# ScalarE takes the exponentials of both halves of query tiles 7 to 17 head by head, with the maximum as its bias

## The chip, the cores and the metric

The kernel runs on one core of a Trainium2 chip. The metric is the device time of one execution in microseconds (us); lower is better. TensorE (PE) multiplies matrices into PSUM, which has eight banks; VectorE (DVE), ScalarE (ACT) and GpSimd (POOL) do the elementwise work, and DMA queues move data.

## The reference

Three stages follow one another on 4 batches of 576 tokens. The first is attention with random features, 8 heads of 64, 128 features; the two others are feed-forward layers, one with a mixing over tokens before it, one with a Fourier transform.

```python
def phi(x):
    proj = np.einsum('bhsd,md->bhsm', x, omega)
    sq = np.sum(x * x, axis=-1, keepdims=True) / 2.0
    h = proj - sq
    h = h - np.max(h, axis=-1, keepdims=True)
    return np.exp(h) / np.sqrt(m)
q_p, k_p = (phi(q_s), phi(k_s))
kv = np.einsum('bhsm,bhsd->bhmd', k_p, v)
z = np.sum(k_p, axis=2)
num = np.einsum('bhsm,bhmd->bhsd', q_p, kv)
den = np.einsum('bhsm,bhm->bhs', q_p, z)[..., None] + 1e-06
attn = num / den
...
h = np.maximum(xt @ w_tok1, 0.0) @ w_tok2        # over tokens, per batch
u = x + h.transpose(0, 2, 1)
x = u + np.maximum(u @ w_ch1, 0.0) @ w_ch2
...
mixed = np.real(np.fft.fft(np.fft.fft(x, axis=1), axis=2))
un = normalised(x + mixed)
out = x + mixed + np.maximum(un @ w2_ch1, 0.0) @ w2_ch2
```

The term `sq` falls out of `phi`, since it is the same for all features of a row and the maximum is taken off.

## The kernel before

The order of all instructions on every engine is written out by hand in the program; each engine works its list in that order and waits on semaphores.

**Attention.** The 2304 tokens are 18 tiles of 128 rows. Keys and queries of a tile are worked in two halves g of four heads. A list `order` sets the sequence of these (kind, tile, half) slots; where both kinds are at hand, key and query slots alternate, and a query tile begins with its half 1. In each slot `project` multiplies the transposed tile with omega (six matmuls, line 506) into one PSUM bank; operands are split into a high and a low part, so that three products make one. `split_in` (493, 494) makes these parts some slots ahead: ScalarE casts, GpSimd subtracts. `feature` (520 to 528) takes the row maxima of the four heads on VectorE, negated, and the exponentials. For one part of the slots VectorE adds the negated maxima over all four heads (`df`, line 527) and ScalarE takes one exponential of 128x512 (528); for the other part ScalarE reads the bank itself, head by head, with the maximum as its bias (524). Three slots later a key half is multiplied with v (540); a query half is turned by TensorE (565), copied by ScalarE (574 or 569), and later multiplied with the sums of the keys (582) and divided on VectorE (595 to 602). ScalarE and GpSimd split the result (608, 609), and TensorE turns it (616).

**Banks.** Two banks have the tag H, four the tag A, two hold numerators (N0, N1). Projections, turned tiles and the products of the token mixing (`tok_mix`, 667 and 680, added to `x2` by VectorE at 683) all take turns on A. The bank of a projection comes free when its last reader is done.

**Between the slots** VectorE widens weights of the next layers from 64-bit words into a high and a low float (`widen`, 341 to 372, with one copy on ScalarE at 348). A budget for each slot sets how many of these steps stand there; they are not tied to a time. When a batch is complete, steps of `tok_mix` are mixed in, one each slot or each second slot.

**After attention** come the channel layer (776, 860, 861, 898), the transform and the second feed-forward layer, which are not touched.

The lines that decide who takes the maximum off:

```python
if kind == "q":
    by_act = g == 0
else:
    by_act = (i + g) % 3 != 0 if i < 5 else i + g > 0
```

Of the kernel before, what the change touches and what calls it, by code (L numbers as in the profile page):

```python
# [302 lines left out]
def mix_kernel(ctx: ExitStack, tc: tile.TileContext, qt, kt, va, om, w1, w2, wch, wff, t1, t2, out):  # L303
# [208 lines left out]
    def feature(kind, i, g):  # L512
        p4 = proj.pop((kind, i, g)).rearrange("p (h m) -> p h m", m=M)

        if kind == "q":
            by_act = g == 0
        else:
            by_act = (i + g) % 3 != 0 if i < 5 else i + g > 0
        mx = e0.tile([128, 4, 1], F32, tag="mx", name="mx")
        dve.tensor_reduce(out=mx, in_=p4, axis=AX.X, op=ALU.max, negate=True)  # L520
        f = e0.tile([128, 4, M], F32, tag="f", name="f", bufs=6)
        if by_act:
            for hh in range(4):
                act.activation(out=f[:, hh], in_=p4[:, hh], func=AF.Exp, bias=mx[:, hh])  # L524
        else:
            df = e0.tile([128, 4, M], F32, tag="df", name="df", bufs=2)
            dve.tensor_tensor(out=df, in0=p4, in1=mx.to_broadcast([128, 4, M]), op=ALU.add)
            act.activation(out=f, in_=df, func=AF.Exp)
        ft[kind, i, g] = f
# [251 lines left out]
    def attention():  # L781
# [35 lines left out]
        for n in range(-1, n_all + LAG_X):  # L817
            while loads and at[loads[0]] <= n + AHEAD_LOAD:
                load(*loads.pop(0))
            if n == n_all:  # L820
                enter_mlp()
            if 0 <= n < n_all:
                project(*order[n])
            sums(n)
            queries(n)
            while splits and at[splits[0]] <= n + AHEAD_SPLIT:
                split_in(*splits.pop(0))
            if 0 <= n < n_all:
                feature(*order[n])
            results(n)  # L830
            if n >= 2:

                side.step(0.0 if n < 6 else SLOT0_US if n < 10 else SLOT1_US if n < 36 else SLOT_US)
            if fill and (len(fill) > 3 or n % 2 == 0):
                fill.pop(0)()
            for fn in early[:3]:
                fn()
            del early[:3]
# [759 lines left out]
```

## Time and profile before

| | before |
|---|---|
| median of 3 runs | 954.01 us (952.9 to 954.3) |
| profiled execution, own time | 953.26 us |
| its span in the trace | 951.2 us |
| TensorE busy | 931.4 us |
| VectorE busy | 644.2 us |
| ScalarE busy | 301.3 us |
| GpSimd busy | 118.8 us |

The span runs from the first to the last instruction of the trace; about 2 us of the execution lie outside it. Busy times count overlapping instructions once. The ends of matmuls are modelled, so a busy TensorE can still stand behind a short wait; VectorE's and ScalarE's rows overlap by about 0.1 us from one to the next, since the end of an instruction covers the landing of its result.

### The profile page before, as it was taken

Reading aid. Unit: us, or ns where it says so; the run is one execution under the profiler, and the core shown is the slowest. Engines: PE = TensorE matmul, PEld = TensorE weight load, DVE = VectorE, ACT = ScalarE, POOL = GpSimd, SP = SyncE. Lnnn points to the kernel's source line nnn. Section 1 sums busy time; section 2 is a strip of 40 time slices with the busy share of each in tenths; the row PEclk is TensorE's granted clock in tenths of the full one; section 3 lists DMA queues with packets and bytes.
Section 4 is the critical chain, followed back from the end, with each engine's and each line's share of the span. In section 5 each row is a group of like instructions: output and inputs, shape, how many; then the busy total and the mean of one; then the engine's idle time right before and its main releaser. Section 6 shows DMA issues by size and latency. Waiting matters only on the chain.

```text
span 951.2 us, 14064 instructions
## 1 busy us (share of the span) xinstructions
PE 931.4 (98%) x5344; PEld 829.7 (87%) x5344; DVE 644.2 (68%) x1270; ACT 301.3 (32%) x676; POOL 118.8 (12%) x110
## 2 busy tenths in 40 slices
PE   7999998989999999999999999999999999999998
PEld 7999898878889988888888888889899998899986
DVE  5987999985776687877864577667565457533342
ACT  5885765742122222212221212212311113311121
POOL 3353343321120122011000000000000000000000
PEclk9999999999999999999999999999999999999999
DMA  8665464388889386584155348739776756687764
GB/s 272 221 211 178 143 231 173 122 318 320 341 352 418 100 341 217 191 292 167 67 177 216 139 147 270 246 126 359 266 244 234 238 183 221 221 263 257 252 205 160
DMA packets 68257, 216.47 MB, mean 228 GB/s; under 512 B 5600, under 2 KB 14432, under 8 KB 54240
## 3 DMA queue, kind: packets, MB, share of 16 engines
q1 hardware_dynamic: 60992, 172.40, 51.9%
q0 software_dynamic: 7056, 43.06, 12.3%
q8 instruction: 42, 0.69, 0.3%
q14 instruction: 23, 0.19, 0.1%
q10 hardware_dynamic: 144, 0.13, 0.1%
HBM read 169.30 MB, written 42.47 MB: 223 GB/s over the span
## 4 chain that ended last, share of the span: by engine, by line
PE 89%; DVE 9%; ACT 1%; issue 0%; DMA 0%; DVEq 0%; ACTq 0%
PE H L776 22%; PE A L898 16%; PE A L1470 14%; PE H L1457 12%; PE A L1264 7%; PE A L506 4%; PE H L540 2%; PE N L582 2%; DVE mx L520 2%; PE A L667 1%; PE S L1077 1%; DVE cvo L364 1%; PE A L565 1%; PE S L1090 1%; DVE x L598 1%; DVE cvo L372 1%
## 5 line engine op out<-in xcount | busy, mean ns | idle before, releaser
L776 PE MATMUL H<-uh,w 128*128 128x512 f32 (+1 forms) x800 | 215.3, 355 | 2.1 <-DVE x L683 2.1
L776 PEld LDWEIGHTS H<-uh,w 128*128 128x128 f32 x800 | 136.5, 189 | 22.2 <-DVE x L683 2.3
L860 ACT ACTIVATE hh<-H 128x512 fp32r<-128x512 f32 (+1 forms) x92 | 49.0, 533 | 270.7 <-PE H L776 270.5
L776 PE MATMUL H<-ul,w 128*128 128x512 f32 (+1 forms) x304 | 113.7, 374 | 0.4 <-DVE ul L763 0.4
L898 PE MATMUL A<-hh,w 128*128 128x512 f32 (+1 forms) x480 | 108.7, 369 | 0.0
L861 DVE SCALAR_TENSOR_TENSOR hl<-H,hh 128x512 fp32r<-128x512 f32 (+1 forms) x92 | 55.8, 606 | 64.5 <-ACT hh L860 64.3
L1470 PE MATMUL A<-w2t,b 128*128 128x512 f32 x384 | 99.3, 394 | 0.0
L898 PEld LDWEIGHTS A<-hh,w 128*128 128x128 f32 x480 | 84.3, 189 | 15.0
L1457 PE MATMUL H<-b,w1t 128*128 128x384 f32 x480 | 91.5, 336 | 0.0
L1457 PEld LDWEIGHTS H<-b,w1t 128*128 128x128 f32 x480 | 85.0, 188 | 4.0 <-DVE tmp L1501 0.3
L1470 PEld LDWEIGHTS A<-w2t,b 128*128 128x128 f32 x384 | 70.6, 188 | 11.7
L524 ACT ACTIVATE f<-A,mx 128x128 f32<-128x128 f32 x204 | 58.9, 395 | 31.1 <-DVE mx L520 23.4
L776 PEld LDWEIGHTS H<-ul,w 128*128 128x128 f32 x304 | 57.4, 189 | 9.9 <-DVE ul L763 0.8
L898 PE MATMUL A<-hl,w 128*128 128x512 f32 (+1 forms) x240 | 59.2, 369 | 0.0
L1264 PE MATMUL A<-w,hh 128*128 128x512 f32 x192 | 50.5, 395 | 0.0
L520 DVE TENSOR_REDUCE mx<-A 128x4 f32<-128x512 f32 x70 | 47.6, 681 | 3.7 <-ACT f L524 2.2
L898 PEld LDWEIGHTS A<-hl,w 128*128 128x128 f32 x240 | 42.7, 189 | 7.6
L540 PE MATMUL H<-v,f 128*128 128x65 f32 x320 | 40.5, 272 | 0.4 <-ACT f L524 0.4
L540 PEld LDWEIGHTS H<-v,f 128*128 128x128 f32 x320 | 39.4, 193 | 0.8 <-ACT f L524 0.6
L1264 PEld LDWEIGHTS A<-w,hh 128*128 128x128 f32 x192 | 34.6, 189 | 6.1
L360 DVE SCALAR_TENSOR_TENSOR cvo<-cvy,cvo 128x1024 int32<-128x1024 int32 (+2 forms) x32 | 39.3, 1228 | 0.5
L1462 ACT ACTIVATE b<-tmp 128x384 fp32r<-128x384 f32 x16 | 8.4, 525 | 98.1 <-DVE tmp L1523 98.1
(261 smaller groups left out, 1703.4 us busy)
## 6 DMA issues: line engine op xcount, KB each, us to landing
w<-kept SPq DMA_DIRECT2D x60, 1024.0 KB, 6.8
w2t<-kept SPq DMA_DIRECT2D x55, 512.0 KB, 4.9
w1t<-kept SPq DMA_DIRECT2D x48, 512.0 KB, 5.0
stg<-in_wff_dram POOLq DMA_DIRECT2D x16, 1024.0 KB, 6.8
kept<-cvo POOLq DMA_DIRECT2D x13, 1024.0 KB, 7.3
stg<-in_wch_dram SPq DMA_DIRECT2D x9, 1024.0 KB, 6.1
kept<-cvo POOLq DMA_DIRECT2D x16, 512.0 KB, 7.7
kept<-so SPq DMA_DIRECT2D x16, 512.0 KB, 7.7
```

The costliest lines, as they stand in the source:

```text
L360: dve.scalar_tensor_tensor(out=st["h"], in0=st["y"].bitcast(I32), scalar=-0x80000000, in1=st["h"], op0=ALU.bitwise_and, op1=ALU.bitwise_or)
L506: pe.matmul(out=pj[:, p_ * 256:p_ * 256 + 256], lhsT=a[:, c, :], rhs=w, start=(n == 0), stop=(n == 2), skip_group_check=True)
L520: dve.tensor_reduce(out=mx, in_=p4, axis=AX.X, op=ALU.max, negate=True)
L524: act.activation(out=f[:, hh], in_=p4[:, hh], func=AF.Exp, bias=mx[:, hh])
L540: pe.matmul(out=kvp[b, g][:, hh * 65:hh * 65 + 65], lhsT=ft["k", i, g][:, hh, :], rhs=src["v", i, int(off > 0)][:, 4 * g + hh, :], start=( ...
L776: pe.matmul(out=hb[:, 0:n], lhsT=w(a, kk), rhs=u[:, kk, 0:n], start=(c == 0), stop=(c == 11))
L860: act.activation(out=hh, in_=hb[:, 0:n], func=AF.Relu)
L861: dve.scalar_tensor_tensor(out=hl, in0=hb[:, 0:n], scalar=0.0, in1=hh, op0=ALU.max, op1=ALU.subtract)
L898: pe.matmul(out=acc[i][:, 0:cols], lhsT=a[:, cs], rhs=v, start=(n == 0 and c_ == 0), stop=(n == NCH - 1 and c_ == 2))
L1264: pe.matmul(out=acc[t], lhsT=a[:, t * 128:t * 128 + 128], rhs=w, start=(n == 0 and c_ == 0), stop=(n == NFF - 1 and c_ == 2))
L1457: pe.matmul(out=to, lhsT=w[:, a, cs], rhs=v[:, q], start=(start and n == 0), stop=(n == 5), skip_group_check=True)
L1470: pe.matmul(out=acc[t], lhsT=h[n // 2][:, t * 128:t * 128 + 128], rhs=w[:, n % 2], start=(begins and n == 0), stop=(ends and n == 2))
```

## The change

For query tiles 7 to 17 the condition is now true for both halves. In those tiles half 1 has no `df` on VectorE any more, and its one exponential of 128x512 on ScalarE becomes four of 128x128 that read the bank. Query tiles 0 to 6 and all key tiles stay as they are.

```diff
         if kind == "q":
-            by_act = g == 0
+            by_act = g == 0 or i > 6
         else:
             by_act = (i + g) % 3 != 0 if i < 5 else i + g > 0
```

On VectorE, at half 1 of query tile 7, in the middle of the token mixing of the first batch (A is a bank, mx the maxima; cvo, cvy and stg are buffers of the widening):

```order
 L683 TENSOR_TENSOR x_655<-A,x_655 128x288
 L520 TENSOR_REDUCE mx<-A 128x4
-L527 TENSOR_TENSOR df<-A,mx 128x512
 L368 TENSOR_SCALAR cvy<-cvo 128x1024
 L341 TENSOR_SCALAR cvy<-stg 128x1024
```

The steps of the widening behind the difference now follow the maximum directly; this is so eleven times, and nothing else moves on VectorE.

On ScalarE, at the same place (xh is the high part of a divided tile, qh of a query tile, qpT a turned one):

```order
 L608 CAST xh<-x 128x512 [waits DVE_49]
 L493 CAST qh<-qs 128x512 [waits DMAHW5_49,PE_49,Pool_49]
-L528 ACTIVATE f<-df 128x512 [waits DVE_49]
+L524 ACTIVATE f<-A,mx 128x128 [waits DVE_49]
+L524 ACTIVATE f<-A,mx 128x128 x3
 L574 COPY qpT<-A 128x512 [waits PE_49]
 L621 COPY x_1192<-N 128x4x128 [waits PE_49]
```

Four instructions stand where one stood; the order around them is the same.

On TensorE, where the bank of that half is used next, by a product of the token mixing:

```order
 L616 MATMUL N<-ident,x 128x128 x3
 L582 MATMUL N<-kvs,qpT 128x65 x4
-L680 MATMUL A<-w2hl,h1h 128x288 [waits DVE_49,PE_49]
+L680 MATMUL A<-w2hl,h1h 128x288 [waits DVE_49,Activation_49]
 L680 MATMUL A<-w2hl,h1h 128x288
 L680 MATMUL A<-w2hl,h1l 128x288
 L680 MATMUL A<-w2hl,h1h 128x288 x2
 L680 MATMUL A<-w2hl,h1l 128x288
-L506 MATMUL A<-om_h,qh 128x256 [waits Activation_49]
+L506 MATMUL A<-om_h,qh 128x256 [waits DVE_49]
```

TensorE's order is the same throughout. The bank is now given back by ScalarE and not by VectorE, and the projection behind it takes a bank that VectorE gives back.

## Rows read from the trace of the kernel before

**Rows 1.** The page, busy time of each engine.

```profile
PE 931.4 (98%) x5344; PEld 829.7 (87%) x5344; DVE 644.2 (68%) x1270; ACT 301.3 (32%) x676; POOL 118.8 (12%) x110
```

**Rows 2.** Windows: length, busy of PE, PEld, DVE, ACT, POOL; clock; DMA.

```profile
87.00:110.50 23.50, 21.87 (x179) 20.86 (x177) 22.98 (x47) 14.34 (x39) 9.20 (x6) 1.00 0.46 158
110.50:136.00 25.50, 25.39 (x190) 23.95 (x191) 23.86 (x44) 17.84 (x44) 9.77 (x6) 1.00 0.62 217
136.00:181.00 45.00, 40.45 (x333) 38.56 (x331) 43.89 (x90) 28.63 (x71) 17.63 (x11) 1.00 0.43 158
215.00:950.00 735.00, 731.81 (x3802) 639.75 (x3800) 455.49 (x881) 158.34 (x312) 38.35 (x47) 1.00 0.66 234
```

**Rows 3.** The chain that ended last: start, length, what; its changes of engine.

```profile
87.11 0.19 DVE rd L596
...
110.46 0.98 PE A L506 x6
...
136.09 0.19 DVE rd L596
...
180.92 0.75 PE A L616 x4
```

**Rows 4.** Line 527 by itself, 80 to 215 us: min/median/max, first to last.

```profile
L527 DVE TENSOR_TENSOR df<-A,mx x9: 691/691/693, 90.6 to 179.6; 128x512 f32<-128x512 f32 x9
L527 DVE TENSOR_TENSOR df<-H,mx x2: 692/692/692, 173.6 to 185.0; 128x512 f32<-128x512 f32 x2
```

**Rows 5.** VectorE in order of time: start, length, instruction, idle before it.

```profile
89.93 0.68 DVE L520 TENSOR_REDUCE mx<-A 128x4 f32<-128x512 f32 x1
90.64 0.69 DVE L527 TENSOR_TENSOR df<-A,mx 128x512 f32<-128x512 f32 x1
91.24 0.68 DVE L368 TENSOR_SCALAR cvy<-cvo 128x1024 int32<-128x1024 int32 x1
91.84 1.78 DVE L341 TENSOR_SCALAR cvy<-stg 128x1024 f32<-128x1024 f32 x1
...
96.95 0.68 DVE L520 TENSOR_REDUCE mx<-A 128x4 f32<-128x512 f32 x1
97.54 0.69 DVE L352 TENSOR_SCALAR cvo<-stg 128x1024 int32<-128x1024 int32 x1
...
109.09 0.69 DVE L341 TENSOR_SCALAR cvy<-stg 128x1024 f32<-128x1024 f32 x1
...
115.35 0.69 DVE L527 TENSOR_TENSOR df<-A,mx 128x512 f32<-128x512 f32 x1
...
140.88 1.79 DVE L341 TENSOR_SCALAR cvy<-stg 128x1024 f32<-128x1024 f32 x1
```

**Rows 6.** ScalarE in order of time.

```profile
90.79 0.62 ACT L493 CAST qh<-qs 128x512 fp32r<-128x512 f32 x1 [2.06 <-POOL xl L609]
91.36 0.63 ACT L528 ACTIVATE f<-df 128x512 f32<-128x512 f32 x1
91.90 0.57 ACT L574 COPY qpT<-A 128x512 f32<-128x512 f32 x1
...
97.67 1.14 ACT L524 ACTIVATE f<-A,mx 128x128 f32<-128x128 f32 x4 [0.89 <-DVE mx L520]
98.68 0.60 ACT L574 COPY qpT<-A 128x512 f32<-128x512 f32 x1
```

**Rows 7.** GpSimd in order of time.

```profile
88.81 1.98 POOL L609 TENSOR_TENSOR xl<-x,xh 128x512 fp32r<-128x512 f32 x1 [0.25 <-ACT xh L608]
91.49 1.58 POOL L494 TENSOR_TENSOR ql<-qs,qh 128x512 fp32r<-128x512 f32 x1 [0.70 <-ACT qh L493]
```

**Rows 8.** TensorE in order of time.

```profile
92.35 0.51 PE L680 MATMUL A<-w2hl,h1h 128*128 128x288 f32 x2
...
110.46 0.39 PE L506 MATMUL A<-om_h,qh 128*128 128x256 f32 x1 [0.56 <-ACT f L524]
...
116.35 0.28 PE L506 MATMUL A<-om_h,qh 128*128 128x256 f32 x1
```

## The prediction

> **What bounds the kernel now.** I read the page first: TensorE is busy for 931 us of 951, VectorE for 644, ScalarE for 301 [rows 1]. That says that the kernel belongs to TensorE, and it is an average over stages, so the windows come next. Behind 215 us TensorE is idle for 3 us in 735 [rows 2]; nothing of the change lies there, and that part can only move as a whole. The eleven differences that go lie between 90.6 and 185.7 us [rows 4]. Three stretches of this time differ. From 87 to 110.5 us VectorE is busy for 22.98 us of 23.50 and TensorE for 21.87; from 136 to 181 us VectorE for 43.89 of 45.00 and TensorE for 40.45; between the two TensorE for 25.39 of 25.50 [rows 2]. The chain of waits says the same by another way: it goes over to VectorE at 87.11 and back to TensorE at 110.46, again to VectorE at 136.09 and back at 180.92 [rows 3]. So in the two outer stretches VectorE's list sets the pace, and TensorE waits for banks that VectorE, or ScalarE right behind a maximum, gives back (as at 110.46 us [rows 8]). TensorE's idle time there, 23.50 - 21.87 = 1.63 and 45.00 - 40.45 = 4.55 us, 6.2 in all, is about what a faster VectorE can give back. The ends of matmuls are modelled, and the first matmul behind a wait is drawn 0.39 us long where the usual one has 0.28 [rows 8]; for some dozen waits that hides another 1.3 us, so the ceiling is 7.5 us.
>
> **What is taken away.** A maximum at 89.93 us is followed by the difference at 90.64 and the next work at 91.24, 1.31 us later; without a difference the next work starts 97.54 - 96.95 = 0.59 us behind the maximum [rows 5]. One difference thus takes 0.72 us of VectorE's list: its 0.60 and 0.12 in which it waits for the maximum to land. Eleven make 7.9 us. Only those in the outer stretches count. Two begin in the first, 1.4 us together. Two, the one at 115.35 us and the next, lie where TensorE has no idle time, and are worth nothing: VectorE will just wait there. Six begin between 136 and 181 us, 4.3 us together; the last, at 185.0 us, lies behind the chain's return to TensorE. (That there are nine on A up to 179.6 and two on H from 173.6 to 185.0 us is in [rows 4]; the places in between follow from the list.)
>
> **What is added.** One exponential of 128x512 keeps ScalarE from 91.36 to 91.90, 0.54 us; four of 128x128 from 97.67 to 98.68, 1.01 us [rows 6]. That is 0.47 us more in each tile, 5.2 in all. ScalarE is busy for 14.34 us of 23.50 and 28.63 of 45.00 in the outer stretches [rows 2]; eight of the eleven longer steps, 3.8 us, stand in these two, which have 25 us free, so by the sum there is room. The result is not later: the old way ended 0.69 + 0.63 us and two hand-overs, together 1.38 us, behind the maximum (90.61 to 91.99), the new one ends 1.18 us behind it (97.63 to 98.81) [rows 5, 6].
>
> The bank is. It was free when the difference ended, 0.72 us behind the maximum (91.33); now it is free with the fourth exponential, 1.18 us behind it, 0.46 us later. At 116.35 us TensorE projects into a bank that a difference freed at 115.35 + 0.69 = 116.04 [rows 5, 8]: 0.31 us of slack, so 0.15 us of new wait. At 92.35 us it takes a bank freed at 91.33, 1.02 us of slack [rows 5, 8]; but ScalarE comes to these exponentials only behind a cast that waits for GpSimd, at 91.36 [rows 6], and they will end at 91.36 + 1.14 = 92.50. That delay of about 0.2 us falls in a stretch where TensorE has idle time ahead, and I count it at nothing; without that cover it would cost the 0.2, here and once more at the like place near 141 us.
>
> For ScalarE's price there is a rule in the Trainium skill, "ScalarE: Activation LUTs", Rules for kernel authors: about 0.3 us for each ACTIVATE and 0.83 ns for each element. As an estimate from that page four of 128 take 1.6 us and one of 512 takes 0.7, a surcharge of 0.9 us where the row has 0.47; the banks would be held 0.5 us longer still, and the sum below would come to about 4.4 us. Successive ACTIVATEs overlap in the rows, which the rule doesn't count.
>
> **The sum.** First stretch: 1.4 - 0.15 = 1.25 us. Second stretch: 4.3 us, of which I take 3.5. The last tiles have no key slots between their own and follow each other closely (three differences from 173.6 to 185.0 us [rows 4]); there ScalarE's 0.47 each falls on a shorter stretch and the banks are wanted sooner; 0.5 for one bank held longer and 0.3 for ScalarE's queue is what I take off, an estimate from the 0.46 and 0.47. Together 4.75 us.
>
> **GpSimd** moves this either way. The widening at 91.84 us takes 1.78 us, and 0.69 us when GpSimd is idle [rows 5]; GpSimd's subtraction begins at 91.49 [rows 7]. It happens once more at 140.88 (1.79 us). The difference and the maximum are not stretched by GpSimd's work up to 90.79 us. Four of the eight differences that count stand ahead of such widening steps, two in each outer stretch, and now the widening runs up against GpSimd at other moments. It can lose the whole 0.72 us, four times, 2.9 us, when it only waits for GpSimd's end instead of for the difference; or it can win 1.1 us twice. At the first place the step at 91.24 would start at about 90.5, wait until 90.79, and the one behind it would begin at about 91.3, 0.2 us ahead of GpSimd's start at 91.49, which is tied to ScalarE's cast and not to VectorE. So I take it to get through, but at a lead of 0.2 us only, and what it wins is capped by TensorE's idle time left (1.63 - 1.25 and 4.55 - 3.5 = 1.4 us). I add 0.6 us, a little under half of that.
>
> The sum is 5.4 us, against the profiled execution 953.26 - 5.4 = 947.9 us; that execution lies 0.75 us under the median of 954.01, so the forecast is 948.6 us. By the bounds of the parts the gain is 4.75 - 2.9 = 1.9 us at least and 7.5 at most.
>
> **Rivals.**
> 1. *Banks come back later.* Every second slot a bank is held 0.46 us longer. Where ScalarE comes late to the exponentials, TensorE waits, and a part of the gain is only moved from VectorE's waits to ScalarE's. For it: the slack of 0.31 at 116.35, and the late start at 91.36. Against it: the other slack of 1.02, and exponentials that now start 0.7 us earlier. If four of the eight tiles of the outer stretches lose 0.5 us, 2 us more are gone: a gain near 3, 951 us.
> 2. *The widening waits for GpSimd instead.* Then the 2.9 us above are lost and rival 1's waits come on top; the gain falls under 1.9 us, and about 953 us is left. For it: 1.1 us of stretch at 91.84 us. Against it: only four of eight places, and there a lead. The Trainium skill, "SBUF — State Buffer", Who interferes with whom, has it that VectorE and GpSimd share one port pair as a lock, held for a whole instruction by whichever issues first. The two stretched rows agree; no run here shows yet who is first when the difference is gone.
> 3. *Slower.* TensorE's list takes the new wait at every one of the eleven banks, and ScalarE's 0.47 us adds to each tile. It decides from the point at which the mean new wait passes 0.5 us, since eleven of them are then as much as the gain on VectorE. If VectorE's lead is worth nothing and each tile costs its 0.47, it ends at 954.0 + 5.2 = 959.2 us. Against it: 16 us in which ScalarE is idle between 136 and 181 us.
> 4. *All of TensorE's idle time goes*, and the gain passes 7.5 us: 946 us.
>
> **Chances.** Forecast, gain between 3.5 and 7.5 us: 0.68. Rival 1: 0.13. Rival 2: 0.10. Rival 3: 0.05. Rival 4: 0.04. A change under 0.2%, 1.9 us, can't be told from none by a measurement of this kernel. Faster are the forecast and rivals 1 and 4, 0.85; same is rival 2, 0.10; slower is rival 3, 0.05. The range reaches from the ceiling, 954.0 - 7.5 = 946.5 us, into rival 1, 951.6 us, and leaves rivals 2 to 4 out.
>
> **What would show it.** In the profile after, the chain should still go to VectorE near 87 and 135 us and back to TensorE earlier by 1 to 2 us and then by 5 in all; TensorE's idle time in the outer stretches should be near 1 us instead of 6.2; the widening behind the first removed difference should take 0.7 us and not 1.78; the channel layer should begin some 5 us sooner and take as long as before. The forecast is wrong if TensorE's waits there are as long as now with ScalarE's exponentials as what ended them, or if the widening is stretched at more places than before.

## The result, and the profile after

| | before | after |
|---|---|---|
| median of 5 runs | 954.12 us (952.9 to 954.3) | 944.42 us (944.04 to 946.03) |
| ratio | | 0.9903, 95% interval 0.9885 to 0.9922 |
| profiled execution, own time | 953.26 us | 946.03 us |
| its span | 951.2 us | 943.9 us |
| TensorE, VectorE, ScalarE busy | 931.4, 644.2, 301.3 us | 930.4, 633.2, 306.4 us |

It is faster by 9.7 us from median to median, where 5.4 were forecast and 7.5 stood as the ceiling; 944.42 us lies below the range. Both kernels have executions of two lengths some 1.6 us apart (after: a mean granted clock of 0.998 in the longer, 0.999 or 1.0 in the shorter), and most of before's runs were of the longer, most of after's of the shorter kind: like against like it is 954.2 against 945.9 and 952.9 against 944.2, 8.3 to 8.7 us.

The windows of the kernel after (busy times in the columns of [rows 2]; its span ends at 943.9 us, inside the last one):

```profile
87.00:110.50 23.50, 23.50 (x202) 23.40 (x201) 23.09 (x47) 17.88 (x50) 12.40 (x8) 1.00 0.46 159
110.50:136.00 25.50, 25.50 (x191) 24.07 (x191) 23.82 (x44) 17.42 (x48) 10.19 (x7) 1.00 0.64 222
136.00:181.00 45.00, 44.75 (x360) 43.17 (x359) 43.54 (x100) 36.50 (x103) 17.70 (x12) 1.00 0.48 179
215.00:950.00 735.00, 724.54 (x3766) 633.04 (x3764) 449.35 (x873) 156.78 (x310) 37.62 (x45) 1.00 0.65 229
```

TensorE was idle for 1.63 and 4.55 us in the two outer stretches [rows 2]; now for 0.00 and 0.25. VectorE is as busy there as it was, but it does more of the program in the time, and TensorE no longer waits for it. The chain of waits no longer goes to VectorE: from 85 to 112 us it names TensorE alone, and only one piece of ScalarE stands in it up to 182 us:

```profile
by line: PE A L506 27.2%; PE A L680 22.7%; PE H L540 18.8%; PE N L582 17.4%; PE A L565 9.7%; PE N L616 4.9%
```

```profile
158.70 0.89 ACT f L524 x3
```

How much TensorE won can be told without the modelled ends, from the starts of the same matmuls. On TensorE after (start, length), those that answer to 92.35, 110.46 and 116.35 [rows 8] and to 180.92 [rows 3]:

```profile
91.94 0.53 PE L680 MATMUL A<-w2hl,h1h 128*128 128x288 f32 x2
...
107.37 0.28 PE L506 MATMUL A<-om_h,qh 128*128 128x256 f32 x1
...
113.26 0.39 PE L506 MATMUL A<-om_h,qh 128*128 128x256 f32 x1
...
171.90 0.55 PE L616 MATMUL A<-ident,x 128*128 128x128 f32 x3
```

From the first to the second it was 18.11 us and is 15.43, 2.68 less; from the third to the fourth 64.57 and 58.64, 5.93 less; between the second and the third 5.89 both times. So the change is worth 8.6 us between these marks. (The lead of 0.41 us at the first is 0.57 that arose ahead of 87 us, where nothing was changed, less 0.16 that TensorE waits there for the bank that ScalarE now gives back.)

Where VectorE's share of it comes from is seen at the first difference that is gone. VectorE after, and then GpSimd after, in order of time:

```profile
89.36 0.68 DVE L520 TENSOR_REDUCE mx<-A 128x4 f32<-128x512 f32 x1
89.96 0.81 DVE L368 TENSOR_SCALAR cvy<-cvo 128x1024 int32<-128x1024 int32 x1
90.70 0.69 DVE L341 TENSOR_SCALAR cvy<-stg 128x1024 f32<-128x1024 f32 x1
91.31 0.43 DVE L683 TENSOR_TENSOR x<-A,x 128x288 f32<-128x288 f32 x1
```

```profile
88.24 1.99 POOL L609 TENSOR_TENSOR xl<-x,xh 128x512 fp32r<-128x512 f32 x1 [0.25 <-ACT xh L608]
90.93 1.59 POOL L494 TENSOR_TENSOR ql<-qs,qh 128x512 fp32r<-128x512 f32 x1 [0.70 <-ACT qh L493]
```

The step behind the maximum starts 0.60 us behind it and not 1.31: the 0.72 of the sum. The next, at 90.70, is 0.23 us ahead of GpSimd's subtraction at 90.93 and takes 0.69 us; before, at 91.84, it came after GpSimd's start at 91.49 [rows 7] and took 1.78 [rows 5]. That is 1.1 us on top of the difference's own 0.72. The opposite happens too, and in the widening steps further on both are seen. VectorE before, then after, the same steps in the same order:

```profile
100.52 1.74 DVE L360 SCALAR_TENSOR_TENSOR cvo<-cvy,cvo 128x1024 int32<-128x1024 int32 x1
...
103.86 1.87 DVE L364 SCALAR_TENSOR_TENSOR cvo<-cvo,stg 128x1024 f32<-128x1024 int32 x1
...
155.57 1.53 DVE L368 TENSOR_SCALAR cvy<-cvo 128x1024 int32<-128x1024 int32 x1
...
161.06 2.04 DVE L372 SCALAR_TENSOR_TENSOR cvo<-cvo,cvy 128x1024 fp32r<-128x1024 f32 x1
```

```profile
98.27 1.94 DVE L360 SCALAR_TENSOR_TENSOR cvo<-cvy,cvo 128x1024 int32<-128x1024 int32 x1
...
101.10 1.34 DVE L364 SCALAR_TENSOR_TENSOR cvo<-cvo,stg 128x1024 f32<-128x1024 int32 x1
...
150.16 0.68 DVE L368 TENSOR_SCALAR cvy<-cvo 128x1024 int32<-128x1024 int32 x1
...
154.07 1.22 DVE L372 SCALAR_TENSOR_TENSOR cvo<-cvo,cvy 128x1024 fp32r<-128x1024 f32 x1
```

Taken over all widening steps of a stretch (the same steps in both kernels), the time beyond an undisturbed step (0.69 us for lines 341, 352, 356 and 368, 1.22 for 360, 364 and 372) was 2.95 us in the first stretch, 2.88 in the middle and 5.25 in the second; after it is 1.67, 4.24 and 3.30. I call this the stretching. In the outer stretches it fell by 1.28 and 1.95 us; in the middle it rose by 1.36, where VectorE has time to spare.

### The profile page after: what moved, and what is told of

Its sections match the earlier page's. It is cut to its first block, busy times and chain, and to the rows that moved or that the text cites. A ratio compares the mean times of both kernels' runs of the same rounds, so it can differ in the third digit from the quotient of the medians.

```text
span 943.9 us, 14085 instructions
## 1 busy us (share of the span) xinstructions
PE 930.4 (99%) x5344; PEld 830.1 (88%) x5344; DVE 633.2 (67%) x1259; ACT 306.4 (32%) x709; POOL 120.7 (13%) x110
## 4 chain that ended last, share of the span: by engine, by line
PE 97%; DVE 2%; ACT 0%; DMA 0%; issue 0%; DVEq 0%; ACTq 0%
PE H L776 23%; PE A L898 16%; PE A L1470 14%; PE H L1457 12%; PE A L1264 7%; PE A L506 6%; PE H L540 4%; PE N L582 3%; PE A L565 2%; PE A L667 1%; PE A L680 1%; PE S L1077 1%; PE S L1090 1%; PE S L680 1%; PE H L667 1%; PE S L667 1%
## 5 line engine op out<-in xcount | busy, mean ns | idle before, releaser
L524 ACT ACTIVATE f<-A,mx 128x128 f32<-128x128 f32 x240 | 69.8, 396 | 23.2 <-DVE mx L520 22.6
```

## The experiments

All are compared by the distances between the marks used above: from the matmul at 92.35 us before to that at 110.46 (first stretch), and from 116.35 to 180.92 (second). "VectorE" is 0.72 us for each difference that is gone there plus the fall of the stretching, "TensorE" what the distance became shorter.

| run | first: VectorE | TensorE | second: VectorE | TensorE | ratio to before, 95% |
|---|---|---|---|---|---|
| the change | 1.44 + 1.28 | 2.68 | 4.32 + 1.95 | 5.93 | 0.9903 (0.9885 to 0.9922) |
| tiles 7, 8 | 1.44 + 1.29 | 2.68 | 0 | 0.12 | 0.9973 (0.9961 to 0.9984) |
| tiles 9, 10 | 0 | 0.01 | 0 | 0.19 | 1.0000 (0.9991 to 1.0008) |
| tiles 11 to 17 | 0 | 0.01 | 4.32 + 2.03 | 5.84 | 0.9946 (0.9933 to 0.9959) |
| differences kept | 0 + 0.02 | 0.22 | 0 + 0.76 | 0.35 | 1.0011 (1.0002 to 1.0020) |
| before, no subtractions | 0 + 2.95 | 2.70 | 0 + 5.25 | 5.85 | 0.9897 (0.9884 to 0.9910) |
| after, no subtractions | 1.44 + 2.95 | 2.68 | 4.32 + 5.25 | 6.98 | 0.9897 (0.9885 to 0.9910) |
| tiles 7, 11 | 0.72 + 0.75 | 1.64 | 0.72 + 0.83 | 1.61 | 0.9966 (0.9954 to 0.9979) |
| tiles 7, 11, work moved | 0 + 0.96 | 1.25 | 0 + 0.96 | 1.11 | 0.9975 (0.9966 to 0.9984) |

**The change in three parts.** One edit each:

```diff
-            by_act = g == 0 or i > 6
+            by_act = g == 0 or i in (7, 8)      # first stretch
+            by_act = g == 0 or i in (9, 10)     # middle
+            by_act = g == 0 or i > 10           # second stretch
```

> Only query tiles 7 and 8, those of the first stretch, give up the difference. Theory A: a stretch gains what VectorE's list loses, 0.72 us for each difference and, besides, what the widening no longer loses to GpSimd (1.28 us in this stretch between the two traces), up to TensorE's gaps from start to start (2.7 us here). A expects 1.4 + 1.3 = 2.7 us, about 951.4 us. Theory B, the sum on record: 1.25 us, 952.9 us, the widening adding little.

> Only query tiles 9 and 10, between the two stretches, give up the difference. A and B: TensorE has no gap there, VectorE only waits there, so 0 us, 954.1 us (a bank wait of 0.13 us at most). Rival: VectorE carries the lead into the second stretch, 1.4 us, 952.7 us.

> Only query tiles 11 to 17 give up the difference; six lie in the second stretch. A: 4.3 us from the differences and 2.3 us of widening no longer stretched are more than TensorE's gaps there, which are 6.0 us from start to start, so 6.0 us, 948.1 us. B: 3.5 us and up to 0.6 of the widening, 950.0 to 950.6 us.

Medians: 950.77, 952.85 and 948.26 us beside 953.39 for before. The two outer parts give what theory A says, 2.68 and 5.84 us, and not the 1.25 and 3.5 of the prediction's sum. The middle part gives nothing, as both had it (ratio 1.0000); of the rival's 1.4 us the second stretch has 0.2. The windows of the kernel with tiles 7 and 8, then those of the one with 11 to 17, show the parts side by side: TensorE's idle time goes where the differences go, and stays elsewhere.

```profile
87.00:110.50 23.50, 23.50 (x201) 23.40 (x201) 23.09 (x46) 17.79 (x50) 12.42 (x8) 1.00 0.46 159
110.50:136.00 25.50, 25.48 (x192) 24.06 (x191) 23.82 (x46) 16.01 (x41) 10.25 (x7) 1.00 0.66 227
136.00:181.00 45.00, 40.40 (x324) 38.04 (x323) 43.86 (x91) 30.06 (x74) 15.86 (x11) 1.00 0.43 159
```

```profile
87.00:110.50 23.50, 21.89 (x178) 20.88 (x177) 23.02 (x46) 14.35 (x39) 9.18 (x6) 1.00 0.47 158
110.50:136.00 25.50, 25.39 (x191) 23.98 (x192) 23.85 (x45) 17.86 (x44) 9.76 (x6) 1.00 0.62 217
136.00:181.00 45.00, 44.79 (x369) 43.63 (x368) 43.66 (x97) 36.43 (x104) 19.77 (x13) 1.00 0.45 165
```

**ScalarE's part alone.**

```diff
         if by_act:
+            if kind == "q" and g and i > 6:
+                df = e0.tile([128, 4, M], F32, tag="df", name="df", bufs=2)
+                dve.tensor_tensor(out=df, in0=p4, in1=mx.to_broadcast([128, 4, M]), op=ALU.add)
             for hh in range(4):
```

> ScalarE takes the exponentials head by head from the bank as in the changed kernel, but VectorE still makes the eleven differences, which nothing reads. A: VectorE's list is as long as before, so no gain, and only two bank waits of 0.13 us: 954.1 to 954.4 us. B: banks held longer and ScalarE's queue cost 0.15 + 0.8 us: 955.1 us. Rival C: the gain comes from exponentials that are ready sooner and not from VectorE's time: 950 us or less.

Median 954.68 us, 1 us slower than before (0.2 to 1.9). So there is no gain while VectorE's list stays as long; A's 0.3 us and B's 1 us both lie in this interval, and between the marks the loss is 0.91 - 0.22 - 0.35 = 0.3 us. TensorE, then ScalarE, at the place of [rows 8], 116.35 us, where the 0.91 arises:

```profile
116.84 0.38 PE L506 MATMUL A<-om_h,qh 128*128 128x256 f32 x1 [0.77 <-ACT f L527]
```

```profile
115.64 1.14 ACT L527 ACTIVATE f<-A,mx 128x128 f32<-128x128 f32 x4 [1.56 <-DVE df L525]
```

From 110.46 to this matmul it takes 0.91 us longer than before. Here the exponentials start only when the kept difference ends (114.92 + 0.69 = 115.61 us), so the bank is held for a difference and four exponentials.

For the same reason this run can't judge rival C: its exponentials are not ready sooner than before. Against C speaks what ended TensorE's waits in the kernel before, from 87 to 181 us (us in total, times, longest):

```profile
PE A L565 <- ACT f L524: 1.7, 2, 1.2
PE A L506 <- ACT f L524: 1.6, 2, 1.1
PE H L616 <- DVE x L598: 0.8, 1, 0.8
PE A L680 <- ACT f L524: 0.5, 2, 0.3
```

The rest of that list is VectorE's (lines 683 and 598). The exponentials that the change makes sooner are those of line 528, and TensorE waited for none of them; those of line 524 waited for VectorE's maxima in their turn (12.0 us from 87 to 182 us). The next run shows the other side: it gains as much with these exponentials left as they were.

**GpSimd's subtractions left out,** from the kernel before and from the changed one. The same edit in both:

```diff
+        if i >= (13 if kind == "k" else 8):
+            act.copy(out=h, in_=t)
+            src[kind, i] = (h, h)
+            return
         l = ld.tile([128, 4, 128], F32R, tag="l", name=kind + "l")
...
         act.copy(out=xh, in_=x[:, 0:DM])
+        if 5 <= i <= 12:
+            xhl[i] = (xh, xh)
+            return
```

> The kernel before without GpSimd's 23 subtractions between 87 and 178 us; the high parts stand in for the low ones, so the results are not the reference's. Theory A, that GpSimd's work stretches the widening and that this time is on the path: the stretched steps (88 to 104 us: 0.69 + 1.10 + 0.52 + 0.65 = 3.0 us; 136 to 171 us: 5.2 us) return to their length, VectorE's list gets 3.0 and 5.2 us shorter, and with TensorE's gaps of 2.7 and 6.0 us the gain is 2.7 + 5.2 = 7.9 us, near 945.5 us, with every difference still in place. Theory B, that the widening adds at most 0.6 us: 952.5 us or more.

> The changed kernel without the same 23 subtractions. A: TensorE's gaps in both stretches are closed already, so nothing more comes: 944.4 us within 0.5, and only 1 us under the kernel before without subtractions. B: the differences are worth their 0.72 us each whatever GpSimd does, so 5 us under that kernel.

943.69 and 944.13 us beside 954.01 for before. With all differences in place the first is as fast as the changed kernel. Its windows in the outer stretches, and VectorE at the place of [rows 5], difference included (line numbers are those of this kernel):

```profile
87.00:110.50 23.50, 23.50 (x203) 23.50 (x202) 22.94 (x51) 17.18 (x44) 0.00 (x0) 1.00 0.52 172
...
136.00:181.00 45.00, 44.24 (x357) 42.68 (x356) 43.91 (x104) 33.31 (x82) 2.83 (x2) 1.00 0.45 173
```

```profile
89.31 0.69 DVE L531 TENSOR_TENSOR df<-A,mx 128x512 f32<-128x512 f32 x1
89.92 0.68 DVE L368 TENSOR_SCALAR cvy<-cvo 128x1024 int32<-128x1024 int32 x1
90.52 0.69 DVE L341 TENSOR_SCALAR cvy<-stg 128x1024 f32<-128x1024 f32 x1
```

The step that took 1.78 us takes 0.69, and over all the widening of the three stretches the stretching is nil. That shows theory A's cause: GpSimd's work stretches VectorE's, 2.95 and 5.25 us of it, and this time was on the path like the differences. The gain is larger than A's: 8.55 us between the marks where A had 7.9, with 5.85 in the second stretch, 0.6 more than the stretching there. The edit also takes away ScalarE's waits for GpSimd (2.06 us at one place of [rows 6]), and its share was not measured apart. Either of the two, the differences or the subtractions, taken away alone, closes nearly all of TensorE's waits. Taking away both brings 1 us over the change between the marks (the second stretch 6.98 instead of 5.93) and nothing that the medians tell; B's 5 us are out.

**Two differences taken out, and the same work put back in another place.** The first of the two is the change for the tiles 7 and 11 alone (`i in (7, 11)`). The second has this besides:

```diff
     def feature(kind, i, g):
...
+        if owed:
+            df = e0.tile([128, 4, M], F32, tag="df", name="df", bufs=2)
+            dve.tensor_tensor(out=df, in0=p4, in1=owed.pop().to_broadcast([128, 4, M]), op=ALU.add)
         mx = e0.tile([128, 4, 1], F32, tag="mx", name="mx")
...
+        if kind == "q" and g and i in (7, 11):
+            owed.append(mx)
```

> Only query tiles 7 and 11 give up the difference, the two whose next widening steps were stretched to 1.78 and 1.79 us. A: 0.72 us for the difference and 1.1 - 0.13 = 0.97 us for the widening in each place, 3.4 us together, none of it capped (gaps of 2.7 and 6.0 us). List alone, without GpSimd: 1.4 us.

> As the run with tiles 7 and 11 alone, but VectorE still does an addition of the same size over a bank, one slot later, ahead of the next maximum, behind the two widening steps; nothing reads its result. VectorE's list is thus as long as before and only the place of 0.69 us in it is another. A: the widening gets ahead of GpSimd all the same, 0.97 us in each place, 1.9 us together. If only the length of VectorE's list counts: 0 us.

950.27 and 951.13 us beside 953.65. VectorE, then GpSimd, in the second kernel:

```profile
89.03 0.67 DVE L525 TENSOR_REDUCE mx<-A 128x4 f32<-128x512 f32 x1
89.63 0.82 DVE L368 TENSOR_SCALAR cvy<-cvo 128x1024 int32<-128x1024 int32 x1
90.37 0.68 DVE L341 TENSOR_SCALAR cvy<-stg 128x1024 f32<-128x1024 f32 x1
90.97 0.44 DVE L690 TENSOR_TENSOR x<-A,x 128x288 f32<-128x288 f32 x1
91.34 0.67 DVE L523 TENSOR_TENSOR df<-A,mx 128x512 f32<-128x512 f32 x1
```

```profile
87.91 1.99 POOL L616 TENSOR_TENSOR xl<-x,xh 128x512 fp32r<-128x512 f32 x1 [0.25 <-ACT xh L615]
90.60 1.59 POOL L494 TENSOR_TENSOR ql<-qs,qh 128x512 fp32r<-128x512 f32 x1 [0.71 <-ACT qh L493]
```

The addition is done, 1.6 us later than where it stood; the widening step is ahead of GpSimd and takes 0.68; the addition itself runs beside GpSimd and takes 0.67 as ever. With as many instructions on VectorE as before, the two stretches are 1.25 and 1.11 us shorter, 2.4 us of the 3.25 us that the two tiles give without the moved work. (0.12 us in each place is the wait for the maximum, which the moved addition no longer has.) That only the length of the list counts, 0 us, is out, and the place is worth more than the work here. The Trainium skill, "SBUF — State Buffer", Who interferes with whom, says which operations of VectorE can meet GpSimd: those with two inputs in SBUF and, in a two-port mode, tensor_scalar; not tensor_reduce, and none with at most one input in SBUF outside that mode. The rows agree: the widening steps (lines 341 to 372) are stretched (1.78 us in [rows 5], 0.82 here), the maximum at 89.03 and the addition at 91.34, which read a bank, take 0.67 beside GpSimd.

**Further versions.** No difference at all (`by_act = True` for all tiles):

> All query and key tiles have their exponentials taken head by head from the bank; VectorE makes no difference at all. A: the ten further differences lie ahead of 87 us, where TensorE has 0.4 us of gaps from 24 to 50 us, so at most 0.4 us is won, 944.0 us. Rival: ScalarE is busy for 23.6 of 26 us there; ten times 0.47 us do not fit, and it ends 2 us slower than the changed kernel, 946.4 us.

944.42 us (ratio 0.9912, 0.9891 to 0.9932), the same as the changed kernel. The rival didn't come: from 24 to 50 us ScalarE is busy for 24.74 of 26 us, and TensorE for 25.51, where it was 25.60 before.

```profile
24.00:50.00 26.00, 25.51 (x219) 25.24 (x220) 24.00 (x51) 24.74 (x78) 10.51 (x8) 1.00 0.78 231
```

What is left of TensorE's waits from 60 to 215 us in the changed kernel (us in total, times, longest) stands at the end of attention:

```profile
PE H L776 <- DVE x L683: 2.1, 1, 2.1
PE N L616 <- DVE x L598: 1.0, 1, 1.0
PE H L776 <- DVE ul L763: 0.4, 1, 0.4
PE A L565 <- ACT f L524: 0.3, 1, 0.3
```

So widening steps were taken out of the end of attention, in three ways (n_all is the number of slots, 72; seven rounds follow the last of them, in which the last tiles are finished, and they are the "last seven slots" below):

```diff
-                side.step(0.0 if n < 6 else SLOT0_US if n < 10 else SLOT1_US if n < 36 else SLOT_US)
+                side.step(0.0 if n < 6 or n >= n_all else ...)                  # last seven
+                side.step(0.0 if n < 6 or n >= n_all + 3 else ...)              # last four
+                side.step(0.0 if n < 6 or n >= n_all else ... n < 32 ...)       # last seven, more from slot 32
```

> The changed kernel, with no new steps of the widening in the last seven slots of attention; they come later, in the channel layer. In the changed kernel TensorE waits 1.0 us at 197.9 and 2.1 us at 202.2 us for work that stands on VectorE behind such steps. A: these 3.1 us go, 941.3 us. Rival: the channel layer's weights come later by as much as was saved, 944.4 us or more.

> The changed kernel, with no new steps of the widening in the last four slots of attention (the earlier run left them out of the last seven). A: the waits of 1.0 and 2.1 us at 197.9 and 202.2 us go in most part, 3 us under the changed kernel, near 941.4 us, and with fewer steps pushed back the times scatter less than from 940 to 949.5 us. Rival: the scatter comes from the steps that are pushed back and stays.

> The changed kernel, with no new steps of the widening in the last seven slots of attention, and the larger budget for a slot from slot 32 on instead of 36, so that half of what is left out at the end is done earlier, where VectorE has room (10 us busy of 17 from 70 to 87 us). A: the 3.1 us of waits at the end go and the weights are as early as before, 941 us with little scatter. Rival: the steps moved ahead make VectorE the bound before 70 us, 18.0 us busy of 20 there, and part of the 3.1 us is lost, 943 us.

Medians 943.29 us (940.07 to 949.51; ratio 0.9910, 0.9881 to 0.9939), 944.56 us (941.27 to 944.85; 0.9905, 0.9890 to 0.9920) and 949.13 us (0.9952, 0.9938 to 0.9966). In the first the waits did go (TensorE is busy for 33.8 of 34 us from 181 to 215 us, and 30.5 in the changed kernel), and the profiled execution is the shortest here, 940.07 us. But neither of the first two has a median that can be told from the change's, so the 941 us that A had for both are not shown. In these few runs the scatter fell with four slots in place of seven, the median didn't; what sets it was not settled.

The third lost, in two places. From 136 to 181 us TensorE gains 2.5 us in its profile on the kernel before, and 5.7 in the changed kernel; the stretching there is 6.1 us, and 3.3 in the changed kernel. Each widening step stands in another slot there, and meets GpSimd elsewhere. The waits that went at the end make up for most of that: at 212 us of the kernel before it is 8.0 us ahead, the changed kernel 9.1 until its clock falls. Then, in the channel layer, TensorE waits for the DMA of a weight up to 273.39 us, its clock falls behind that wait, and the lead at the end is 4.2 us:

```profile
PE H L776 <- DMA w<-kept: 2.0, 1, 2.0
```

That is the cost that the first of the three had as its rival, weights that come later; why this one came late was not tried.

## Why the prediction was right in direction and too small in size

- **Where the time comes from: right.** VectorE set the pace in the two outer stretches, its removed work became TensorE's, and the two tiles in the middle were worth nothing.
- **0.72 us for a difference, 1.4 and 4.3 us: right** (0.60 us from the maximum to the next step instead of 1.31).
- **GpSimd, "+0.6 us": the term that failed.** It measured 1.28 + 1.95 = 3.2 us. The mechanism was stated and its first place foreseen to the detail: the step at 91.24 is held up a little by GpSimd (0.81 us long and not 0.69) and the next gets ahead by 0.2 us (0.23). What I did wrong was to count only two stretched steps, 91.84 and "once more at 140.88", and to hold the winnings down to what I took for TensorE's remaining idle time, 1.4 us. The trace of the kernel before has eleven stretched steps in the outer stretches; others of them (103.86, 155.57 and 161.06 us) changed as well. They lost it 8.2 us, more than the differences that went there (5.8).
- **The ceiling of 7.5 us: mis-sized.** Idle time of 6.2 us in the windows stands for at least 8.6 by the starts of matmuls. I counted some dozen waits and 0.11 us hidden in each; 15 waits closed, and 8.6 us came back while the idle time in the windows fell by 6.18 - 0.25 = 5.9, so 0.18 us was hidden in each. The run without differences and without subtractions closed 2.68 + 6.98, so even 8.6 was not all.
- **Banks and ScalarE's queue: foreseen in part, and 0.8 us for the second stretch was too much.** There a wait of 0.16 us for a bank is seen at 138.21 us and one of 0.3 us behind an exponential at 158.7. The 0.15 at 116.35 came: the matmul at 113.26 is drawn 0.39 us long, as one behind a wait, and starts 5.89 us behind the mark before it, where the kernel with tiles 7 and 8 alone, which waits at neither mark, takes 5.76. (The kernel before has 5.89 too, because there the earlier of the two marks stands behind a wait.) The 0.2 at 92.35, counted at nothing, came as 0.16. The run with the differences kept shows when such waits would have been dear: 0.9 us at one bank.
- **ScalarE's price: right.** The four exponentials start at 90.75 and the copy behind them at 91.76, 1.01 us in the trace after; ScalarE's busy time rose by 5.1 us, 5.2 in the sum. The estimate of 1.6 us, worked out from the Trainium skill, "ScalarE: Activation LUTs", Rules for kernel authors, is not what this row has.
- **The rivals.** The fourth, given 0.04, is what happened. Put together afterwards, with what the trace after shows of the stretching and the waits, the same sum is 1.44 + 1.28 + 4.32 + 1.95 - 0.16 - 0.3 = 8.5 us, and the marks show 8.6. How far the stretching falls is known from the trace after alone; the trace before shows that 8.2 us of it were there.
- **What would show it.** The widening behind the first removed difference did as written (0.69 us). The chain did not: it was to go to VectorE still, and from 85 to 182 us it doesn't go there at all. TensorE's idle time is 0.25 us and not near 1. The work behind 181 us moved by 9.0 us and not 5, and took as long as before but for the clock (below). "Stretched at more places than before" was no sign of being wrong: from 87 to 181 us 16 steps are longer than usual by over 0.05 us, where it was 15 before, while in the outer stretches the same number, eleven, lost 5.0 us and not 8.2.

## What to carry to other kernels

Before pricing an instruction that goes, list every step on the same engine that is longer than its usual length, add up the excess over the stretch, and look at which engine runs at those moments. Here that sum was larger than the work removed, and moving one instruction behind its neighbours was worth 1.1 to 1.3 us without removing anything. Work that changes the rhythm between VectorE and GpSimd has to be priced over all later meetings and not at the next one alone; the sum before tells how much there is to win, and not how much of it a change will win. Take the ceiling from the starts of matmuls across waits, not from idle time, when their ends are modelled.

## What was not expected of the hardware

- Removing either VectorE's differences or GpSimd's 23 subtractions, which run beside VectorE's work, gave the same ratio within the noise, 0.9903 and 0.9897; removing both gave 0.9897.
- In the changed kernel's profile TensorE's granted clock is at the lower of its two levels (1.2 of 2.4 GHz) from between 202 and 203 to 206 us, right after its longest wait there, 2.1 us up to 202.22, behind one of 1.0 us up to 197.90; at 206 it is at the higher again. The matmuls of line 776 follow each other there in 0.43 us and not in 0.22, and 1.6 us of the lead of 9.1 are gone by 215 us:

```profile
203.00:204.00 1.00, 1.00 (x4) 0.81 (x3) 0.97 (x3) 0.00 (x0) 0.00 (x0) 0.50 1.06 410
206.00:207.00 1.00, 1.00 (x6) 0.83 (x5) 0.72 (x2) 0.15 (x1) 0.54 (x1) 1.00 0.97 410
```

The same fall, behind a longest wait of 2.0 to 2.2 us, is in four more profiles: with the differences kept (behind 212 us), the change without subtractions (202), tiles 7 and 11 alone (209) and the third version of the end (273). It is not in those of the kernel before and six others, which have the same wait of 2.1 to 2.2 us, nor in the two versions of the end without such a wait. What decides it was not tried.
